# Casts and copies moved from GpSimd to VectorE and ScalarE, with a new order of all queues, in an attention and maxout kernel

## The chip, the cores and the metric

The kernel runs on one core of a Trainium2 chip. The metric is the time on the device in microseconds (us), the median of several runs; lower is better. The engines of the core are TensorE (PE in the profile; its weight loads have a row of their own, PEld), VectorE (DVE), ScalarE (ACT), GpSimd (POOL) and SyncE (SP), which only issues DMAs here. Each works through its own queue in order, and they wait for each other by semaphores.

## The reference, cut to what matters

```python
# attention, for 4 batches x 8 heads x 768 positions x 64
scores = (q @ k.T) / 8 + bias          # bias: -slope[head] * distance
keep   = (key < 8) | (0 <= query - key < 96)
a      = softmax(where(keep, scores, -1e9))
x      = (a @ v), heads side by side   # 3072 x 512
# maxout
h      = max(x @ w1, x @ w2, x @ w3)   # 3072 x 768
out    = h @ w_out                     # 3072 x 512, f32
```

A query sees the 8 first keys and the last 96 before it, so a tile of 128 queries needs the keys of its own tile, of the tile before it, and the 8 global ones. All inputs are f32 in HBM; the kernel computes in bf16 with f32 sums.

## The kernel before, in words

The 3072 positions are 24 tiles T of 128 (6 per batch); G is a pair of tiles. The tiles are put together to 7 chunks c of 4, 2, 2, 4, 4, 4 and 4 tiles (`SIZES`), and the maxout part runs over chunks. The whole program is one list, `SCHEDULE`, in which each word is a unit: a letter, its numbers, and after `@` the place in a ring of buffers (for units on PE the PSUM bank) that it takes. Line 571 goes through the list and emits each unit's instructions, so the order of the list is the order within each engine's queue; there is no other scheduling. A last number often names the engine: 0 ScalarE, 1 VectorE, 2 GpSimd (`copies`, line 190). The units are:

- `l` loads q, k or v of a pair of tiles (512 KB), with 12 as the pair's number for the first four tiles, in parts; `w` and `q` load weights; all on SP's queue
- `c` (L195 on VectorE and ScalarE, L201 in two halves on GpSimd) casts q or k to bf16; `v` (L254) casts one half of a tile's v; `W` and `Q` (L195, L201) cast weights
- `x` (L270, L276) transposes q or k by matmuls into PSUM, `y` (L283, L287) copies that out; `X` (L292) does both by a DMA
- `G` (L313, L315) and `V` (L321 to L325) put the 8 global keys and values into the rows of a tile that the next tile's queries no longer need; a `V` must come after the product `A` that reads the old rows. On GpSimd `V` copies 32-bit words, elsewhere bf16
- `S` (L349) scores, `e` (L356) exp from PSUM on ScalarE, `m` (L365, L367) product with a mask on VectorE. With `b` (L335) ahead of `S`, the bias is added by matmuls instead and there is no `m`; `B`, `K` and `R` make the bias and the masks at the start
- `A` (L391, L394) weights times v, with a column of ones that gives the sums; `n` (L402, L403) normalises on VectorE
- `t` (L418) and `u` (L421) transpose x by matmuls and copy it out; `Z` (L424) does it by a DMA
- `F` (L433) is one of 18 products per chunk (6 blocks f, 3 weights j), 4 matmuls each into one PSUM bank. `f` is its way out: j = 0 copies to bf16 (L447, ScalarE or VectorE), j = 1 and 2 take the maximum on VectorE (L449, L452)
- `O` (L457) is the last product of one tile, 6 matmuls of 512 columns; `o` (L471) copies it to SBUF, `s` (L477) stores it. `s` with a last number 2 stores in two halves
- `E` (L479 to L505) is the end of the last chunk in one unit: its four tiles with copies and stores, the last tile in parts of 256, 128 and 128 columns, the last of them stored from ScalarE's queue. Behind `E` the list has one more tile, `O5.0@2 o5.0.0@5 s5.0.2`
- `D` (L532) is matmuls on zeros whose result nobody reads: ten of 512 columns at the start, and three of 256 after the first transposes

`RINGS` says how many buffers each kind has; a unit that takes a place waits until the last readers of it are done.

Of the kernel before, what the change touches and what calls it, by code (L numbers as in the profile page):

```python
# [24 lines left out]
    l0.12.1@0 l1.12.1@1 D10.512@0 l1.12.3@2 l0.12.2@3 l0.12.3@4 R K7 K6 B1.1 K4 B2.1 K2 B3.0 K1 K5 B0.1 B6.1  # L25
    K0 c0.12.3.2@0 l1.12.2@5 c0.12.1.1 B4.1 B5.1 c1.12.1.1@1 K3 x12.0.1@0 y0.0.1.0@0 B7.1 l2.0.2@0 D3.256@1
    x12.1.1@1 b0.1@2 v1.0.2 l2.1.2@1 c1.12.3.1 v1.1.2 b1.0@4 y0.1.1.0 b1.1@6 S1.1.1 l0.2.2@6 c0.12.2.1
    y1.0.1.1@1 y1.1.1.0 x12.0.2@0 e1.1@0 c1.12.2.1 x12.0.3 y0.0.0.1 l1.2.2@0 y1.0.0.1 x12.1.3@1 x12.1.2
    y0.1.0.0 S0.1.1 e0.1@1 G0.1 b2.1@6 v2.0.2 v3.0.2 w1.0@0 S1.0.1 G1.0 e1.0@2 b2.0@2 w0.0@0 y1.1.0.1 S2.1.1
    w1.1@1 S0.0.0@0 e0.0@3 l2.2.2@2 S2.0.1 v0.0.1 e2.0@4 w0.1@1 v0.1.1 m0.0.1 e2.1@5 v2.1.2 b3.0@4 A1@0  # L30
    V1.1.1 V1.0.2 G2.1 v3.1.2 w0.2@2 A0@2 S3.0.1 e3.0@6 b3.1@6 n1@0 c0.2.2.2@2 S3.1.1 G3.0 A2@0 V2.0.2
    e3.1@7 V2.1.2 n0@1 t0@2 W0.0.2 c1.2.2.1 u0.0@0 x2.1.2@3 y2.1.2.0@2 w1.2@2 x2.0.2@2 A3@4 t1@6 u1.0 n2@2
    y2.0.2.1 t2@7 n3@3 l0.3.2@1 l1.3.2@2 S4.1.0@0 V3.1.2 e4.1@0 V3.0.2 S4.0.0@2 W1.1.2 u2.1 t3@6 G4.1 u3.0
    W2.0.1 S5.1.0@4 e5.1@2 S5.0.0@0 e5.0@1 m4.1.1 W1.0.1 e4.0@3 F0.5.0@7 F0.4.0@6 W2.1.0 F0.3.0@4 f0.3.0.0@0
    F0.2.0@5 f0.4.0.1@1 F0.1.0@6 v4.1.2 v4.0.2 l2.3.2@0 f0.1.0.0@2 q2@0 v5.1.0 F0.0.0@0 F0.5.1@1 F0.4.1@4
    F0.2.1@6 m4.0.1 f0.0.0.0@3 v5.0.0 f0.5.0.0@4 m5.1.1 A4@2 V4.1.0 F0.3.1@0 W0.1.2 f0.4.1.1 W0.2.0 m5.0.1
    f0.5.1.1 F0.0.1@1 F0.1.1@4 V4.0.1 W1.2.0 n4@1 t4@7 A5@2 W2.2.0 c1.3.2.2@0 f0.0.1.1 f0.1.1.1 F0.1.2@1
    n5@0 u4.1@1 f0.1.2.1@0 F0.0.2@4 q0@1 t5@7 u5.0 q1@2 f0.3.1.1 f0.0.2.1 F0.2.2@2 F0.3.2@3 f0.3.2.1
    c0.3.2.0 f0.2.0.0@2 f0.2.1.1 F1.2.0@4 F1.0.2@7 Q2.0 v7.1.2 F1.0.0@5 f1.0.0.1@3 v6.1.2 F1.0.1@3 f0.2.2.1
    f1.0.1.1 f1.2.0.1@0 Q0.2 f1.0.2.1@1 x3.1.2@6 y3.1.2.1@3 F0.4.2@5 f0.4.2.1 l1.4.2@3 v6.0.2 Q1.2 F1.1.0@0  # L40
    F1.2.2@1 l0.4.2@4 l1.6.2@5 F1.2.1@4 f1.2.1.1 F1.3.1@2 f1.2.2.1 F1.3.2@3 v7.0.2 F1.3.0@4 f1.3.0.0@2
    f1.3.1.1 f1.3.2.1 x3.0.2@1 F0.5.2@5 f0.5.2.1 F1.4.0@2 F1.1.1@3 f1.1.0.0@3 y3.0.2.0 S6.0.0@0 S6.1.0@4
    G6.2 c1.4.2.2@1 c0.4.2.2 l0.5.2@0 c0.5.2.2@2 f1.1.1.1 f1.4.0.0@1 e6.0@4 S7.0.0@6 S7.1.0@2 l1.5.2@6
    c1.5.2.2 e6.1@5 c1.6.2.2@0 e7.1@6 F1.4.1@0 e7.0@7 l2.4.2@1 O0.2@1 f1.4.1.1 m7.1.1 x4.1.2@0 F1.5.2@2
    F1.5.0@3 m7.0.1 v8.1.2 F1.5.1@4 A7@6 f1.5.0.1@0 m6.1.1 m6.0.1 o0.2.0@0 y4.1.2.0@0 f1.5.1.1 f1.5.2.1
    x4.0.2@3 y4.0.2.0 G7.0 l0.6.2@1 c0.6.2.2 F1.4.2@5 O0.1@4 f1.4.2.1 n7@2 o0.1.1@1 A6@0 l2.5.2@2 S8.1.0@2
    S8.0.0@6 n6@3 V7.1.1 G8.1 v8.0.2 F1.1.2@4 O0.3@5 t6@0 v11.0.2 v9.0.2 v9.1.2 f1.1.2.1 V7.0.0 t7@1 e8.1@0
    e8.0@3 S9.0.0@2 u6.0@2 S9.1.0@6 m8.1.1 u7.1 o0.3.0@2 O0.0@4 e9.1@1 m8.0.1 o0.0.0@3 e9.0@2 F2.4.0@5
    m9.1.1 f2.4.0.0@2 A8@0 V8.0.2 n8@1 F2.5.0@4 F2.2.1@6 f2.5.0.1@4 F2.1.0@7 f2.1.0.0@0 G9.0 F2.5.1@5 V8.1.2
# [15 lines left out]
    X16@1 o3.3.0@8 A15@0 n15@2 O3.0@7 S19.1.0@0 v17.1.1 m18.0.1 S16.1.0@2 m18.1.1 e19.1@1 S16.0.0@4 O3.2@6
    o3.0.1@9 e16.0@2 V15.1.2 A18@0 e16.1@6 n18@0 o3.2.1@10 m16.1.1 X17 O3.1@7 G16.0 Z14 o3.1.0@11 m16.0.1
    V15.0.1 S17.0.0@0 v16.0.0 Z12 S19.0.0@2 Z15 e19.0@7 S17.1.0@4 e17.1@0 m17.1.1 F4.4.0@6 e17.0@5 l0.11.2@1
    s1.0 l2.10.2@0 F4.2.0@7 l1.10.2@2 F4.1.0@2 F4.5.0@3 v16.1.0 F4.3.0@0 A16@4 f4.2.0.0@2 Z18@2 V16.1.2
    f4.3.0.0@0 v20.0.2 G18.0 F4.1.2@1 f4.1.0.1@3 c0.11.2.2@1 m17.0.1 v17.0.1 l2.11.2@2 n16@3 s3.1 f4.5.0.0@4
# [542 lines left out]
```

## Time and profile before

| what | value |
|---|---|
| median of 3 runs | 176.07 us (176.06 to 176.23) |
| span of the profiled execution | 174.8 us |
| PE busy | 165.9 us, 95% |
| VectorE busy | 131.9 us, 75% |
| ScalarE busy | 95.4 us, 55% |
| GpSimd busy | 54.7 us, 31% |
| HBM read and written | 25.17 MB and 6.29 MB |

The span runs from the first to the last instruction of one profiled execution; the time of a run has about 1.3 us more around it. A row of the groups reads: line, engine, operation, output<-input, shape, count | busy us, mean ns of one | idle time before them, with what ended it. Matmuls are pipelined, so their durations are longer than their spacing: PE's busy time tells where it has work, not how well it is used.

### The profile page before, as it was taken

What the parts mean: (1) busy time and instruction counts of PE and PEld (TensorE: products, weight loads), DVE (VectorE), ACT (ScalarE), POOL (GpSimd) and SP (SyncE); (2) the same over time, 40 slices, a digit from 0 to 9 for tenths busy, and PEclk for the clock granted to TensorE, in tenths of its full rate; (3) what the DMA queues carried; (4) which work ended last, traced back from release to release, by engine and by line L of the source; (5) the groups of instructions that cost most, each with busy time, mean ns of one, the idle gap of its engine ahead of it and who ended that gap; (6) DMA issues with size and microseconds to landing.
All of it is one profiled execution on the core that took longest, in us unless ns stands there. A gap on an engine that the chain in (4) does not pass through costs nothing.

```text
span 174.8 us, 3865 instructions
## 1 busy us (share of the span) xinstructions
PE 165.9 (95%) x1485; PEld 93.6 (54%) x1507; DVE 131.9 (75%) x268; ACT 95.4 (55%) x147; POOL 54.7 (31%) x99
## 2 busy tenths in 40 slices
PE   7997999999999999898999999999999999999991
PEld 2555745577676877544445545544445554444460
DVE  7889864988599897989898678899578993074910
ACT  5988897672868788440667688200345651402051
POOL 4049295057586717003730003240530000000000
PEclk9999999999999999999999999999999999999998
DMA  5999999999899899999996759998990046370035
GB/s 149 352 292 327 402 360 385 270 371 311 229 303 179 139 183 266 267 290 284 165 135 112 114 145 306 305 210 260 231 213 20 0 120 137 121 286 4 0 119 185
DMA packets 66403, 37.36 MB, mean 214 GB/s; under 512 B 24144, under 2 KB 61392, under 8 KB 66384
## 3 DMA queue, kind: packets, MB, share of 16 engines
q1 hardware_dynamic: 66240, 37.04, 83.3%
q8 instruction: 12, 0.20, 0.5%
q10 hardware_dynamic: 144, 0.07, 0.1%
q14 instruction: 7, 0.06, 0.1%
HBM read 25.17 MB, written 6.29 MB: 180 GB/s over the span
## 4 chain that ended last, share of the span: by engine, by line
PE 76%; DVE 10%; DMA 6%; ACT 3%; issue 2%; SPq 0%; DVEq 0%
PE psum L433 44%; PE psum L457 17%; PE psum L349 6%; DMA xT<-xb 3%; DMA rawqk<-in_k_dram 3%; DVE P L365 3%; PE psum L391 3%; PE psum L394 2%; PE psum L276 2%; DVE ht L452 1%; DVE xb L403 1%; ACT P L356 1%; PE psum L270 1%; DVE qb L195 1%; PE psum L335 1%
## 5 line engine op out<-in xcount | busy, mean ns | idle before, releaser
L433 PE MATMUL psum<-xT,w 128*128 128x512 bf16 (+1 forms) x491 | 97.5, 348 | 1.5 <-DMA xT<-xb 0.7
L433 PEld LDWEIGHTS <-w 128*128 128x128 bf16 x504 | 47.6, 98 | 42.9 <-DMA xT<-xb 0.9
L356 ACT ACTIVATE P<-psum 128x1024 bf16<-128x1024 f32 (+1 forms) x48 | 43.3, 954 | 10.4 <-PE psum L349 10.3
L449 DVE TENSOR_TENSOR h<-h,psum 128x512 bf16<-128x512 bf16 (+1 forms) x42 | 25.0, 605 | 15.9 <-PE psum L433 12.4
L457 PE MATMUL psum<-wo,ht 128*128 128x512 bf16 (+2 forms) x147 | 33.4, 362 | 0.5
L447 ACT CAST h<-psum 128x512 bf16<-128x512 f32 (+1 forms) x27 | 13.8, 523 | 33.1 <-PE psum L433 29.8
L452 DVE TENSOR_TENSOR ht<-h,psum 128x512 bf16<-128x512 bf16 (+1 forms) x42 | 26.2, 644 | 2.1 <-PE psum L433 0.9
L365 DVE TENSOR_TENSOR P<-P,wmask 128x1024 bf16<-128x1024 bf16 x34 | 25.2, 752 | 2.0 <-ACT P L356 1.7
L457 PEld LDWEIGHTS <-ht 128*128 128x128 bf16 x156 | 13.8, 98 | 13.5 <-DVE ht L452 0.2
L254 POOL CAST va<-rawv 64x512 bf16<-64x512 f32 x28 | 18.5, 668 | 4.8 <-DMA rawv<-in_v_dram 3.7
L323 POOL COPY va<-vaf 4x260 int32<-4x260 int32 x17 | 7.2, 424 | 34.9 <-PE psum L394 34.5
L403 DVE TENSOR_TENSOR xb<-psum,rz 128x512 bf16<-128x512 f32 x24 | 16.6, 692 | 0.8
L201 POOL CAST qb<-rawk 128x512 bf16<-128x512 f32 x12 | 7.5, 654 | 23.7 <-DMA rawk<-in_k_dram 23.7
L349 PE MATMUL psum<-qkT 64*128 64x128 bf16 x352 | 14.4, 217 | 0.5 <-DVE qkT L315 0.4
L391 PEld LDWEIGHTS <-P 128*128 128x128 bf16 x192 | 12.6, 97 | 3.2 <-ACT P L356 0.4
L349 PEld LDWEIGHTS <-qkT 64*128 64x128 bf16 x352 | 10.0, 94 | 7.9 <-issue 5.9
L391 PE MATMUL psum<-va,P 128*128 128x65 bf16 x160 | 12.7, 193 | 0.7 <-DVE ht L452 0.6
L447 DVE CAST h<-psum 128x512 bf16<-128x512 f32 (+1 forms) x15 | 9.1, 615 | 5.1 <-PE psum L433 5.1
L471 ACT COPY staging<-psum 128x512 f32<-128x512 f32 x14 | 8.2, 592 | 8.8 <-PE psum L457 8.8
L201 POOL CAST qb<-rawq 128x512 bf16<-128x512 f32 x14 | 8.9, 664 | 9.0 <-DMA rawq<-in_q_dram 5.0
L394 PEld LDWEIGHTS <-P 128*128 128x128 bf16 x160 | 10.5, 97 | 2.1 <-issue 0.7
L394 PE MATMUL psum<-va,P 128*128 128x65 bf16 x128 | 9.9, 193 | 0.0
(72 smaller groups left out, 120.6 us busy)
## 6 DMA issues: line engine op xcount, KB each, us to landing
rawv<-in_v_dram SPq DMA_DIRECT2D x12, 512.0 KB, 7.0
out_dram<-staging SPq DMA_DIRECT2D x21, 256.0 KB, 2.7
rawq<-in_q_dram SPq DMA_DIRECT2D x10, 512.0 KB, 7.1
rawk<-in_k_dram SPq DMA_DIRECT2D x10, 512.0 KB, 7.3
staging<-in_moe_w_dram SPq DMA_DIRECT2D x3, 1024.0 KB, 9.3
staging<-in_moe_w_dram SPq DMA_DIRECT2D x3, 512.0 KB, 8.8
staging<-in_moe_w_out_dram SPq DMA_DIRECT2D x3, 512.0 KB, 6.3
out_dram<-staging SPq DMA_DIRECT2D x5, 128.0 KB, 2.2
```

The costliest lines, as they stand in the source:

```text
L254: copies[how](heads(va(T))[64 * e:64 * e + 64, :, 0:D], src)
L349: nc.tensor.matmul(sp[:, hh, j2, ds], qT(T - ds, 1, hsl, jp), qT(T, 0, hsl, jp), start=not how, stop=True, skip_group_check=True)
L356: nc.scalar.activation(P[:, :, 0:n], sps[T, g].rearrange("p a b d n -> p (a b) d n")[:, :, 0:n], AF.Exp, bias=0.0, scale=scale)
L365: mul(P, P, wmask[:, g, :, 0:2])
L391: nc.tensor.matmul(o, P[:, i, 0], heads(va(T))[:, h], start=True, stop=(t == 0), skip_group_check=True)
L394: nc.tensor.matmul(o, P[:, i, 1], heads(va(T - 1))[:, h], start=False, stop=True, skip_group_check=True)
L403: nc.vector.tensor_tensor(out=x.rearrange("p (g h) d -> p g h d", g=2), in0=o4[:, :, :, 0:64], in1=rz[:, :, :, None].to_broadcast([128, 2, ...
L433: nc.tensor.matmul(ps, w123[f // 2][:, j, dm, (f % 2) * 128:(f % 2) * 128 + 128], xT[c][:, dm], start=(dm == 0), stop=(dm == 3))
L447: copies[how](h01, ps)
L449: nc.vector.tensor_max(h01s[c, f], h01s[c, f], ps)
L452: nc.vector.tensor_max(dst, h01s[c, f].rearrange("p (t e i) -> p t e i", e=2, i=64), ps.rearrange("p (t e i) -> p t e i", e=2, i=64))
L457: nc.tensor.matmul(po, ht[c][:, f, tt * 128:(tt + 1) * 128], wo[:, f, cols], start=(f == 0), stop=(f == NF - 1))
```

## The change

Every unit that named GpSimd now names VectorE or ScalarE, and the list is written anew from the first word to the last: loads, casts, transposes, products and stores come in another order and take other places. GpSimd keeps only what the setup does (iota and the identity). The count of units by letter is the same but for one more `b` (b0.0, so tile 0 loses an `m`), one `D` less, and the units of the end. By engine (ACT, DVE, POOL; before, then after):

| unit | before | after |
|---|---|---|
| `v` | 6, 10, 32 | 20, 28, 0 |
| `c`, whole (1024 columns) | 4, 3, 13 | 11, 9, 0 |
| `c`, of the first four tiles | 0, 5, 1 | 2, 4, 0 |
| `V` | 4, 11, 17 | 15, 17, 0 |
| `G` | 9, 8, 3 | 11, 9, 0 |
| `W` and `Q` | 5, 2, 5 | 7, 5, 0 |
| `u` | 6, 3, 0 | 3, 6, 0 |
| `f` with j = 0 | 27, 15, 0 | 29, 13, 0 |
| `o` (`E` apart) | 14, 6, 0 | 15, 11, 0 |

`E` is gone. `O` can now name a range of blocks f and of 64-column parts, `o` and `s` a range of parts, and the end is made of such units. The rings change as the diff shows. The diff, with the list cut to its first and last lines:

```diff
 SCHEDULE = """
-    l0.12.1@0 l1.12.1@1 D10.512@0 l1.12.3@2 l0.12.2@3 l0.12.3@4 R K7 K6 B1.1 K4 B2.1 K2 B3.0 K1 K5 B0.1 B6.1
-    K0 c0.12.3.2@0 l1.12.2@5 c0.12.1.1 B4.1 B5.1 c1.12.1.1@1 K3 x12.0.1@0 y0.0.1.0@0 B7.1 l2.0.2@0 D3.256@1
...
-    F6.5.0@1 f6.5.0.1@2 F6.5.2@5 f6.5.1.1 f6.5.2.1 E@7 O5.0@2 o5.0.0@5 s5.0.2
+    l0.12.1@0 l1.12.1@1 D10.512@0 l0.12.3@2 R B2.1 B5.1 B1.1 K6 K3 K0 K4 l1.12.2@3 K5 B3.0 B6.1 l1.12.3@4
+    c0.12.1.1@0 B4.1 x12.0.1@0 c1.12.1.1@1 B7.1 B0.1 K7 K2 c0.12.3.0 y0.0.1.0@0 K1 l0.12.2@5 l2.0.2@0 w0.0@0
...
+    o5.1.0@9 s5.1 o6.3.0.4.0@6 o5.2.1@10 s5.2 s6.3.0.4 O6.2@0 o6.2.0@5 s6.2 O5.0@1 o5.0.0@4 s5.0
 """
-RINGS = {'r': 7, 'rv': 3, 'qb': 3, 'qkT': 4, 'sp': 2, 'h': 8, 'P': 8, 'xb': 4, 'xT': 3, 'wst0': 3, 'wst1': 3, 'ht': 2, 'h01': 5, 'rz': 4, 'os': 12}
+RINGS = {'r': 7, 'rv': 3, 'qb': 2, 'qkT': 3, 'sp': 2, 'h': 8, 'P': 7, 'xb': 3, 'xT': 2, 'wst0': 3, 'wst1': 3, 'ht': 2, 'h01': 8, 'rz': 3, 'os': 12}
...
-    def u_O(slot, c, tt):
-        pos[c, tt] = ring("h", slot, [128, DM], FP32, "po")
-        f2_mm(pos[c, tt], c, tt, range(NF))
+    def u_O(slot, c, tt, f0=0, f1=NF, c0=0, c1=8):
+        if slot is not None:
+            pos[c, tt, c0] = ring("h", slot, [128, (c1 - c0) * 64], FP32, "po")
+        for f in range(f0, f1):
+            nc.tensor.matmul(pos[c, tt, c0], ht[c][:, f, tt * 128:(tt + 1) * 128], wo[:, f, c0 * 64:c1 * 64],
                              start=(f == 0), stop=(f == NF - 1))
+    def u_o(slot, c, tt, *rest):
+        c0, c1 = rest[:-1] or (0, 8)
+        osts[c, tt, c0] = ring("os", slot, [128, DM], FP32, "ost")[:, 0:(c1 - c0) * 64]
+        copies[rest[-1]](osts[c, tt, c0], pos[c, tt, c0])
+    def u_s(slot, c, tt, c0=0, c1=8, queue=0):
         T = chunks[c][tt]
+        (nc.sync, nc.scalar)[queue].dma_start(out=out[T * 128:(T + 1) * 128, c0 * 64:c1 * 64], in_=osts[c, tt, c0])
...
-    def u_E(slot):
...
```

The stretch of the new list up to its first products, of which the prediction speaks:

```
...
v3.1.0 S2.0.1 G2.0 b3.0@0 b3.1@4 S3.0.1 S3.1.1 e2.0@1 A2@6
V2.0.1 G3.1 V2.1.1 v3.0.0 e3.1@3 e3.0@0 x2.0.2@2 t0@3 y2.0.2.0@0 t1@4 u1.0@0 u0.0 c1.2.2.1 x2.1.2@5 n2@0
y2.1.2.1 A3@0 n3@1 S4.1.0@6 e4.1@0 S4.0.0@4 G4.1 t2@3 u2.1 e4.0@3 W2.0.0 t3@2 u3.1 S5.0.0@0 e5.0@1 S5.1.0@6
e5.1@2 F0.1.0@2 f0.1.0.0@0 v5.1.0 W1.0.1 F0.3.0@3 F0.0.0@4 f0.3.0.0@1 v4.1.1 v4.0.1 m4.0.1 V3.1.1 F0.5.0@5
...
```

More of the change, by code (lines that the diff above doesn't have):

```diff
@@ L30 @@
[L30 to L49, printed above, removed]
@@ L65 @@
[L65 to L69, printed above, removed]
@@ new lines @@
+    m19.0.1 A15@2 n15@0 Z15 V15.1.1 V15.0.0 O3.2@4 o3.2.1@0 v16.1.1 v17.0.0 S16.1.0@2 S16.0.0@0 O3.3@6 X21@0
+    o2.0.0@1 O3.0@7 e16.1@1 X20 l0.11.2@0 e16.0@2 G16.0 o3.0.0@2 S17.0.0@0 m16.1.1 v19.0.1 o3.3.1@3 l1.11.2@6
+    S19.1.0@2 e19.1@5 S17.1.0@4 e17.1@6 G18.0 G19.0 v18.0.1 m16.0.1 v18.1.1 s3.1 F4.5.0@6 F4.4.0@7 F4.2.0@2
+    f4.2.0.0@3 v16.0.1 A16@4 V16.1.0 e17.0@1 V16.0.0 m17.1.1 v19.1.1 m19.1.1 n16@0 s3.2 l2.11.2@0 F4.0.0@3
+    f4.4.0.1@0 f4.5.0.1@6 F4.1.0@2 A19@4 n19@1 Z19@1 f4.1.0.0@7 m18.1.1 F4.3.0@7 f4.3.0.0@1 F4.4.1@2 f4.4.1.1
@@ L133 @@
         chunks.append(list(range(first, first + n)))
-    last = len(chunks) - 1
     pools = {}
@@ L453, in u_f @@
                                  ps.rearrange("p (t e i) -> p t e i", e=2, i=64))
-    def f2_mm(po, c, tt, fs, cols=slice(0, DM)):
-        for f in fs:
-            nc.tensor.matmul(po, ht[c][:, f, tt * 128:(tt + 1) * 128], wo[:, f, cols],
-                             start=(f == 0), stop=(f == NF - 1))
-    def f2_out(po, ost, c, tt, copy, cols=slice(0, DM), dma=nc.sync):
-        T = chunks[c][tt]
-        copy(ost, po)
-        dma.dma_start(out=out[T * 128:(T + 1) * 128, cols], in_=ost)
```

118 lines of the change are left out of this document (50 added, 68 removed).

## The prediction

> **What bounds the kernel now.** I read the page first, then the sums by stretch, then TensorE's (PE's) own waits.
>
> ```profile
> span 174.8 us, 3865 instructions
> PE 165.9 (95%) x1485; PEld 93.6 (54%) x1507; DVE 131.9 (75%) x268; ACT 95.4 (55%) x147; POOL 54.7 (31%) x99
> ```
>
> ```profile
> core 0: us, PE busy (x) PEld busy (x) DVE busy (x) ACT busy (x) POOL busy (x), PEclk, DMA share, GB/s
> 0.00:22.00 22.00, 19.26 (x236) 11.35 (x238) 18.77 (x55) 18.38 (x31) 9.37 (x23) 1.00 1.01 305
> 22.00:62.00 40.00, 39.72 (x398) 26.44 (x403) 31.09 (x63) 28.78 (x44) 24.72 (x40) 1.00 1.05 280
> 62.00:125.00 63.00, 61.05 (x528) 33.02 (x536) 52.77 (x100) 31.88 (x49) 17.84 (x32) 1.00 1.00 219
> 125.00:165.00 40.00, 39.73 (x288) 19.54 (x292) 27.63 (x50) 13.53 (x20) 2.75 (x6) 1.00 0.39 108
> 165.00:175.00 10.00, 6.10 (x40) 3.23 (x39) 1.64 (x3) 2.88 (x6) 0.00 (x0) 0.92 0.37 133
> ```
>
> From 22 us to 165 us TensorE is busy for 140.5 of 143 us: it is the bound, and its matmuls are the same before and after the change. What can move is the time in which it has nothing to do. That is in three places: the first 22 us, where VectorE (DVE, 18.77) and ScalarE (ACT, 18.38) are both nearly full and the first product F waits for both; a few holes in the middle; and the tail after the last matmul. The two largest holes in the middle are these:
>
> ```profile
> PE psum L433 <- DMA xT<-xb: 0.7, 1, 0.7
> PE psum L391 <- DVE ht L452: 0.6, 1, 0.6
> ```
>
> The start ends here; the columns are start, length, instruction:
>
> ```profile
> 20.11 0.41 DVE L421 COPY xT<-psum 128x512 bf16<-128x512 bf16 x1
> 20.95 0.58 ACT L421 COPY xT<-psum 128x512 bf16<-128x512 bf16 x1
> 21.58 7.93 PE L433 MATMUL psum<-xT,w 128*128 128x512 bf16 x35
> ```
>
> The last transposed activations leave ScalarE at 21.53, and the first F starts 0.05 us later. So whatever is queued ahead of these copies on DVE and ACT sets the start of the long run of matmuls.
>
> **The change: what moves where.** GpSimd (POOL) loses all its work past the setup: 32 v casts, 13 c casts of q and k and one half, 5 weight casts, 17 V copies and 3 G copies. Durations:
>
> ```profile
> L254 DVE CAST va<-rawv 64x512 bf16<-64x512 f32 x8 | 3.4, 423 | 0.1
> L254 ACT CAST va<-rawv 64x512 bf16<-64x512 f32 x4 | 2.5, 618 | 0.0
> L195 DVE CAST w<-staging 128x1024 bf16<-128x1024 f32 x2 | 1.4, 686 | 0.0
> L195 ACT CAST w<-staging 128x1024 bf16<-128x1024 f32 x4 | 4.0, 1042 | 0.0
> L325 DVE COPY va<-vaf 4x520 bf16<-4x520 bf16 x11 | 4.2, 381 | 0.9 <-PE psum L394 0.8
> L325 ACT COPY va<-vaf 4x520 bf16<-4x520 bf16 x4 | 2.5, 621 | 7.9 <-PE psum L394 7.9
> L365 DVE TENSOR_TENSOR P<-P,wmask 128x1024 bf16<-128x1024 bf16 x34 | 25.2, 752 | 2.0 <-ACT P L356 1.7
> L421 DVE COPY xT<-psum 128x512 bf16<-128x512 bf16 x3 | 1.2, 412 | 0.0
> L421 ACT COPY xT<-psum 128x512 bf16<-128x512 bf16 x6 | 3.5, 585 | 3.0 <-PE psum L418 3.0
> L471 DVE COPY staging<-psum 128x512 f32<-128x512 f32 x6 | 4.1, 684 | 0.2 <-PE psum L457 0.2
> L471 ACT COPY staging<-psum 128x512 f32<-128x512 f32 x14 | 8.2, 592 | 8.8 <-PE psum L457 8.8
> L449 DVE TENSOR_TENSOR h<-h,psum 128x512 bf16<-128x512 bf16 (+1 forms) x42 | 25.0, 605 | 15.9 <-PE psum L433 12.4
> L356 ACT ACTIVATE P<-psum 128x1024 bf16<-128x1024 f32 (+1 forms) x48 | 43.3, 954 | 10.4 <-PE psum L349 10.3
> ```
>
> Counting letters in both queues, DVE gains 18 v (18 x 0.423 = 7.6), 6 c of a full 1024 columns less one half (3.7), 3 weight casts (2.1), 6 V (2.3), 3 whole o (2.1) and 3 u (1.2), and gives away 2 first maxout copies and 1 mask product (-1.7): +17.3 us. ACT gains 14 v (8.7), 7 full c (7.3) and two halves (1.2 by the 585 ns of a 512-wide copy), 11 V (6.8), 2 weight casts (2.1) and 2 maxout copies (1.0), and loses 3 o and 3 u (-3.6): +23.5 us.
>
> **What DVE gets back.** While POOL reads SBUF, the mask product can be held up:
>
> ```profile
> 107.98 0.61 POOL L254 CAST va<-rawv 64x512 bf16<-64x512 f32 x1 [0.18 <-DMA rawv<-in_v_dram]
> 108.54 1.16 POOL L201 CAST qb<-rawq 128x512 bf16<-128x512 f32 x2
> ```
>
> ```profile
> 108.19 2.86 DVE L365 TENSOR_TENSOR P<-P,wmask 128x1024 bf16<-128x1024 bf16 x2
> ```
>
> Two products take 2.86 us there, just as long as POOL is at work, and
>
> ```profile
> L365 DVE TENSOR_TENSOR P<-P,wmask x34: 672/685/2058, 21.1 to 141.5; 128x1024 bf16<-128x1024 bf16 x34
> ```
>
> says that the median is 685 and the longest 2058. Mean less median gives 34 x 0.067 = 2.3 us; I take 4 us for all kinds together, between 2.3 and the 5 us that it would be if V copies and early casts lose as much again. So DVE goes from 131.9 to about 145 us, ACT from 95.4 to about 119. [...]
>
> **The first stretch (0 to 22 us).** Up to its last copy of x transposed, DVE's queue now holds one c cast of k or q more (0.69) and one quad half less (-0.42), 3 v (1.27), 3 V (1.14, or 0.86 without POOL beside them), W0.0 (0.69), one u (0.41), one y (0.69) and one G (0.2) more, and one mask product less (-0.4): +4 us on a queue that ended at 20.52. DVE was idle for 22 - 18.77 = 3.2 us of the stretch, into which some of this can fit, at most about 2.3 (the rest lies before its first instruction); of the 4 us of locks, POOL's share of busy time here (9.37 of 54.68) gives 0.7. Bounds: 20.5 + 4 - 2.3 - 0.7 = 21.5, and 20.5 + 4 - 0.7 = 23.8. On ACT, two quad halves (1.2) and 3 v (1.9) are new, an exp (-0.95), a u (-0.6) and a y (-0.6) are gone: +0.9 on a copy that ended at 21.53, which gives 22.4 where it finds no idle time. I take 22.3, just under ACT's 22.4 and near the middle of DVE's bounds: first F **+0.7 us** (-0.1 to +2.2).
>
> ```profile
> 16.54 0.73 DVE L195 CAST qb<-rawk 128x1024 bf16<-128x1024 f32 x1
> ```
>
> On the DMA queue w0.0 (512 KB) now stands ahead of the last q, k and v of this stretch: at 305 GB/s they land 1.7 us later. Behind the cast c1.2.2 on DVE stand n2, n3, u2 and u3, so F would wait; that cast ran at 16.54 without a wait, its data can be there by 18.2, and DVE reaches it at about 19 (22.3 less these four). Hidden, by 0.8 us. The extra bias unit b0.0 is two short matmuls (+0.2 with what it delays); three fill-in matmuls go, which nothing waits for.
>
> **The second stretch (first F to 62 us).** PE's units here come to the same work, some 38 us. DVE holds 9 v (3.8), 4 c (2.7), 4 weight casts (2.7), 6 V (2.3), 2 mask products (1.5) more and about 3 maxout steps less (-1.9): +11 on 31.09 busy us, less 1 to 2 of locks: **40 to 41 us of work in 40 us**. ACT goes to 28.8 + 4 = 33. Back to back, instructions overlap a little, and eight PSUM banks let PE run some F ahead, so a full DVE is no stall by itself; but the 9 us in which it could wait for exp results or matmuls are gone, and each wait is handed on to PE. Bounds: nothing, if the order never leaves DVE waiting, and 4 us, if it waits half as long as it did. I take **+1.2 us**, nearer to nothing because the banks stand between.
>
> **The third stretch (62 to 125 us).** DVE +9 - 2 = 59.5 of 63 us; ACT gains 9 V (5.6), 7 v (4.3), 4 c (4.2), 5 exps that the new order puts here (4.8): 52 of 63. PE lost 1.95 us here, 1.25 in the two named holes, both behind a DVE queue that locks had lengthened. I take **-0.7 us**: the holes go in part, the load is higher (-1.4 to +1.5). New waits: V must wait for the products A that read the old rows.
>
> ```profile
> POOL va L323 <- PE psum L394: 34.5, 7, 10.4
> ACT va L325 <- PE psum L394: 7.9, 2, 6.7
> ```
>
> On POOL these 34.5 us had only other casts behind them; on ACT and DVE the exps, first copies h and maxout steps stand behind a V, and PE waits for them. I cost this at nothing beyond the terms above, since in the queue each V stands behind its A. The rings of xb, xT, qb and qkT lose a place each: n15 must wait until the transposing DMA of tile 14 has read its buffer, with m and f steps behind it on DVE.
>
> ```profile
> xT<-xb SPq DMA_TRANSPOSE x15, 3.4
> ```
>
> Ahead of n15 stand about six DVE units, some 4 us, which cover 3.4; without that cover it is 1 us or so.
>
> **The tail.** The change speaks of a 128-column part last, but both queues end with O5.0, its ScalarE copy and its store; the 128-column part of tile 23 now comes some 12 units before the end. Only the halving of the last store goes:
>
> ```profile
> 171.80 0.81 SPq L477 DMA_DIRECT2D out_dram<-staging x2
> ```
>
> ```profile
> out_dram<-staging SPq DMA_DIRECT2D x21, 256.0 KB, 2.7
> ...
> out_dram<-staging SPq DMA_DIRECT2D x5, 128.0 KB, 2.2
> ```
>
> Before: 171.80 + 0.41 + 2.2 = 174.4; one store of 256 KB: 171.80 + 2.7 = 174.5. **Nothing** (-0.1 to +0.5).
>
> **The sum.** +0.7 + 0.2 + 1.2 - 0.7 + 0 = +1.4 on the profiled span of 174.8, so 176.2; 176.07 - 174.8 = 1.3 us lie around the span in the median of the runs shown, so **177.5 us**. Lowest ends: -0.1 + 0 + 0 - 1.4 - 0.1 = -1.6, 174.5; highest: 2.2 + 0.2 + 1.8 (all ends do not come together: of the 4 + 1.5 of the later stretches I take a third) = +4.2, 180.3.
>
> **Rivals.** *A, VectorE stays the bound into the third stretch* (0.17): the stretch at 40 to 41 of 40 us starts late, its backlog isn't worked off at 94% load, and V waits at the head of ACT's queue hold up exps: 0.7 + 0.2 + 2.0 in the second and 0.8 in the third stretch = +3.7, 179.8. For it speaks the load; against it that the banks have hidden most of DVE's waits so far (PE 39.72 of 40). *B, faster, by the end of the locks* (0.26): place: the start, 66 to 83 and 107 to 111 us; price: the 4 us of locks, of which the 1.25 us of holes have reached PE, and little at the start: 176.07 - 1.2 = 174.9. It decides once the first F starts no later than 21.6 and DVE's work in the second stretch comes in order without waits. Against it: 17 us of new work for 4 us of locks. *C, no difference* (0.08): late start and filled holes cancel: 176.1. *D, the clock* (0.03):
>
> ```profile
> 5.47 0.94 PE L270 MATMUL psum<-identb,qbq 128*128 128x128 bf16 x8
> 6.25 0.49 PE L532 MATMUL psum<-zeros 128*128 128x256 bf16 x3
> 6.99 0.62 PE L270 MATMUL psum<-identb,qbq 128*128 128x128 bf16 x8 [0.25 <-DVE qbq L195]
> ```
>
> Eight transposes take 0.94 us, later ones 0.62, and the three matmuls on zeros between them are removed. If PE fell back to the slow rate in that hole, each early group of transposes would cost 0.32 more; with two such groups ahead of F that is +0.6 beyond the forecast, 178.1. [...] The forecast has the rest, 0.46.
>
> **Range and chances.** 174.5 to 180.3 takes in B and A; outside it lie the worst of A and a B that also shortens the start. A measurement of this kernel tells about 0.2%, 0.35 us, from no change. Faster is B, 0.26; same is C, 0.08; slower is the forecast, A and D, 0.66.
>
> **What would show it.** No POOL instruction beyond the setup; mask products all near 0.69; DVE about 145 and ACT about 119 busy us; first F at 22.0 to 23.0; in 22 to 62 us DVE over 37 us busy and PE with holes that wait for DVE or ACT; the tail 3.6 us after the last matmul as now. I am wrong if the first F starts before 21.6, or if PE's holes between 22 and 125 us stay under 2 us although DVE is full.

## The result and the profile after

The kernel after takes **181.27 us** (median of 4 runs, 180.79 to 183.29) against 176.15 before: 1.0327 times as long, 95% interval 1.0267 to 1.0386. The forecast of 177.5 had the sign, but the time lies 1 us above the top of its range. Runs far above the fastest of the same kernel are left out of all ratios here, so a median can stand higher than its ratio says.

The profiled execution of after took 180.79 us. From its page: the span, the busy time by engine, the shares of the chain that ended last, and the mask products.

```profile
span 179.0 us, 3802 instructions
...
PE 166.4 (93%) x1484; PEld 93.3 (52%) x1506; DVE 141.8 (79%) x305; ACT 118.0 (66%) x180; POOL 1.8 (1%) x9
...
PE 68%; DVE 12%; DMA 11%; issue 3%; SPq 3%; ACT 0%; DVEq 0%
...
L358 DVE TENSOR_TENSOR P<-P,wmask 128x1024 bf16<-128x1024 bf16 x34 | 22.5, 684 | 2.7 <-ACT P L349 2.5
```

The change did what it says. GpSimd has only its setup left, VectorE has 10 us more work and ScalarE 22.6, and the mask products went from a mean of 752 to 684 ns, the longest from 2058 to 694: the delays beside GpSimd's work, which the prediction calls locks, are gone. TensorE has the same work, in a span 4.2 us longer. Its busy time by stage (stretch, length, PE, PEld, DVE, ACT, POOL, clock, DMA) stands beside the table that the prediction shows of before:

```profile
0.00:22.00 22.00, 17.28 (x210) 9.99 (x210) 18.57 (x57) 18.48 (x33) 1.76 (x9) 1.00 1.00 290
22.00:62.00 40.00, 39.63 (x393) 25.14 (x395) 37.33 (x84) 34.26 (x46) 0.00 (x0) 1.00 1.01 287
62.00:125.00 63.00, 59.41 (x571) 33.66 (x579) 54.09 (x110) 50.07 (x79) 0.00 (x0) 1.00 0.99 205
125.00:165.00 40.00, 39.74 (x262) 19.33 (x266) 27.74 (x50) 12.55 (x20) 0.00 (x0) 1.00 0.34 106
```

PE is 2.0 us less busy in the first stretch (17.28 against 19.26, of which 0.5 are the matmuls on zeros that the change takes out), level in the second although VectorE is full there, and 1.6 us less busy in the third. Busy time is no measure of progress, so the same can be counted in columns of matmuls done, from the traces: at 0.216 us for 512 columns, after lies some 1.6 us behind before from 22 to 70 us (1.3 to 2.0), 3.0 at 82 us, 3.9 at 110 us, and no further from there on. So the loss has two places, the start and the stretch from 78 to 110 us. The first F starts here:

```profile
23.40 1.47 PE L426 MATMUL psum<-xT,w 128*128 128x512 bf16 x5
```

That is 1.8 us later than before (21.58). In the third stretch PE's waits have two new heads, at 82 and at 106 us:

```profile
PE psum L384 <- DVE h L442: 1.7, 1, 1.7
...
PE psum L426 <- DVE P L358: 1.1, 1, 1.1
```

The first of them can be followed back by hand. First PE, then VectorE's queue in front of it:

```profile
77.78 2.75 PE L426 MATMUL psum<-xT,w 128*128 128x512 bf16 x12
82.25 0.20 PE L384 MATMUL psum<-va,P 128*128 128x65 bf16 x1 [1.72 <-DVE h L442]
```

```profile
74.86 0.42 DVE L442 TENSOR_TENSOR h<-h,psum 128x256 bf16<-128x256 bf16 x1
78.61 0.42 DVE L247 CAST vaf<-rawv 64x512 bf16<-64x512 f32 x1 [3.33 <-DMA rawv<-in_v_dram]
79.05 0.43 DVE L360 TENSOR_TENSOR P<-P,wmask 128x512 bf16<-128x512 bf16 x1
79.39 1.29 DVE L358 TENSOR_TENSOR P<-P,wmask 128x1024 bf16<-128x1024 bf16 x2
...
81.17 0.43 DVE L360 TENSOR_TENSOR P<-P,wmask 128x512 bf16<-128x512 bf16 x1
81.51 0.68 DVE L442 TENSOR_TENSOR h<-h,psum 128x512 bf16<-128x512 bf16 x1
```

The cast v12.1 stands at the head of VectorE's queue and waits 3.33 us for its load. Four mask products and a maximum that PE needs stand behind it. Before, that cast was on GpSimd. How GpSimd's queue waited for loads in the kernel before:

```profile
POOL qb L201 <- DMA rawk<-in_k_dram: 23.7, 5, 10.1
POOL qbq L201 <- DMA rawqq<-in_q_dram: 5.9, 1, 5.9
POOL qb L201 <- DMA rawq<-in_q_dram: 5.0, 4, 2.1
...
POOL va L254 <- DMA rawv<-in_v_dram: 3.7, 5, 1.9
```

With its other waits that is 85 us, and nothing but casts and copies stood behind them. These rows suggested the theory that most runs below try: **what costs is less the work than the waits that came with it** (W). Its rival is the work itself (L).

### The profile page after: what moved, and what is told of

It is laid out like the page before. It is cut to its first block, busy times and chain, and to the rows that moved or that the text cites. A ratio compares the mean times of both kernels' runs of the same rounds, so it can differ in the third digit from the quotient of the medians.

```text
span 179.0 us, 3802 instructions
## 1 busy us (share of the span) xinstructions
PE 166.4 (93%) x1484; PEld 93.3 (52%) x1506; DVE 141.8 (79%) x305; ACT 118.0 (66%) x180; POOL 1.8 (1%) x9
## 4 chain that ended last, share of the span: by engine, by line
PE 68%; DVE 12%; DMA 11%; issue 3%; SPq 3%; ACT 0%; DVEq 0%
PE psum L426 44%; PE psum L453 13%; DMA rawv<-in_v_dram 11%; PE psum L342 4%; PE psum L384 3%; PE psum L387 2%; DVE ht L445 2%; SPq L222 2%; DVE h L442 2%; DVE va L247 2%; DVE P L358 1%; PE psum L269 1%; DVE qb L188 1%; DVE xb L396 1%; DVE vaf L247 1%
## 5 line engine op out<-in xcount | busy, mean ns | idle before, releaser
L426 PE MATMUL psum<-xT,w 128*128 128x512 bf16 (+1 forms) x489 | 99.0, 348 | 1.9 <-DVE P L358 1.1
L453 PE MATMUL psum<-wo,ht 128*128 128x512 bf16 (+2 forms) x149 | 32.7, 362 | 0.5 <-issue 0.2
L459 ACT COPY staging<-psum 128x512 f32<-128x512 f32 (+1 forms) x15 | 8.4, 573 | 27.4 <-PE psum L453 23.7
L358 DVE TENSOR_TENSOR P<-P,wmask 128x1024 bf16<-128x1024 bf16 x34 | 22.5, 684 | 2.7 <-ACT P L349 2.5
L440 ACT CAST h<-psum 128x512 bf16<-128x512 f32 (+1 forms) x29 | 14.6, 523 | 8.3 <-PE psum L426 4.5
L318 ACT COPY va<-vaf 4x520 bf16<-4x520 bf16 x15 | 9.3, 621 | 5.4 <-PE psum L387 5.2
L440 DVE CAST h<-psum 128x512 bf16<-128x512 f32 (+1 forms) x13 | 7.9, 622 | 5.6 <-PE psum L426 5.6
L247 ACT CAST va<-rawv 64x512 bf16<-64x512 f32 x18 | 11.1, 619 | 0.3
L459 DVE COPY staging<-psum 128x512 f32<-128x512 f32 (+1 forms) x11 | 6.5, 613 | 4.6 <-PE psum L453 2.2
L247 DVE CAST va<-rawv 64x512 bf16<-64x512 f32 x22 | 9.3, 423 | 0.5 <-DMA rawv<-in_v_dram 0.2
```

The source lines that it names most:

```text
L247: copies[how](heads(va(T))[64 * e:64 * e + 64, :, 0:D], src)
L358: mul(P, P, wmask[:, g, :, 0:2])
L426: nc.tensor.matmul(ps, w123[f // 2][:, j, dm, (f % 2) * 128:(f % 2) * 128 + 128], xT[c][:, dm], start=(dm == 0), stop=(dm == 3))
L440: copies[how](h01, ps)
L453: nc.tensor.matmul(pos[c, tt, c0], ht[c][:, f, tt * 128:(tt + 1) * 128], wo[:, f, c0 * 64:c1 * 64], start=(f == 0), stop=(f == NF - 1))
```

## The experiments

Each ratio is to the kernel before on the same chip. The first four expectations were written before W and L had their names and explain their own theories.

| run | median us | ratio (95%) | span, profiled |
|---|---|---|---|
| e1 engines alone | 196.52 | 1.116 (1.111 to 1.121) | 194.7 |
| e2 order alone | 185.19 | 1.052 (1.045 to 1.059) | 182.0 |
| e5 the 44 that never waited | 188.59 | 1.072 (1.066 to 1.078) | 185.7 |
| e6 the 27 that waited | 189.55 | 1.078 (1.074 to 1.082) | 187.9 |
| e4 one load early | 182.35 | 1.026 (1.021 to 1.031) | 178.7 |
| e7 two loads early | 180.93 | 1.026 (1.019 to 1.032) | 181.6 |
| e8 three casts on GpSimd | 182.56 | 1.034 (1.027 to 1.042) | 178.7 |
| e10 third stretch | 181.61 | 1.027 (1.019 to 1.036) | 177.6 |
| e13 third stretch, n15 | 180.14 | 1.020 (1.013 to 1.027) | 178.6 |
| e3 start on GpSimd | 182.45 | 1.037 (1.033 to 1.040) | 181.2 |
| e12 first weight later | 185.15 | 1.053 (1.046 to 1.061) | 182.8 |
| e14 e12 and e13 together | 184.68 | 1.048 (1.041 to 1.055) | 182.6 |
| e15 both at the start | 184.01 | 1.046 (1.042 to 1.050) | 182.1 |
| e17 all | 182.85 | 1.036 (1.028 to 1.044) | 179.2 |
| e18 all, q2 with its own buffer | 179.91 | 1.022 (1.018 to 1.025) | 177.7 |
| e16 before, three casts moved | 176.30 | 1.002 (1.000 to 1.004) | 174.2 |

### The two halves of the change (e1, e2)

e1 is the kernel before with 71 units on the engines that after gives them; e2 is after with the same 71 back on GpSimd.

```diff
-v1.0.2 V1.0.2 c1.3.2.2@0
+v1.0.1 V1.0.1 c1.3.2.0@0
```

> The kernel before, with its own order, rings and end, but each of the 71 units that named GpSimd on the engine that the changed kernel gives it (VectorE or ScalarE). Theory Q (casts and copies do harm at the head of queues that TensorE needs, where they wait for loads and for products): 181 to 186 us, with idle VectorE or ScalarE in front of v, c and V, as the order was not made for it. Rival O (the new order is what costs, the engines are nearly free because the locks go): 175.5 to 177.5 us.

> The changed kernel with its new order, rings and end, but the 71 units that were GpSimd's in the kernel before are GpSimd's again. Theory Q: the holes of TensorE near 80 and 105 us shrink or go and the first product starts near 22.0: 176 to 178.5 us. Rival O (the order costs): 180 to 181.5 us, the holes stay where they are.

Both theories missed both runs. The engines alone cost 20.5 us, more than any estimate, and the order alone 9.2; together they cost 5.1. So the new order belongs to the new engines: it gives back some 15 of the 20.5 us, and it is bad for the old ones. At the start of e1 the granted clock is lower too: 1.00 from 10 to 20 us in before, where PE is busy for 8.98 of the 10 us, and 0.66 in e1:

```profile
10.00:20.00 10.00, 6.80 (x69) 4.04 (x69) 6.09 (x14) 5.85 (x11) 0.00 (x0) 0.66 1.14 335
```

### Waits or work (e5, e6)

The 71 units of e1, split by whether GpSimd waited at that unit in the profile of before.

> The kernel before, in its old order. Of its 71 casts and copies on GpSimd, only the 44 that began there without a wait (29 us of work: 27 v, 10 V, 3 c and 4 others) go to the engines that the kernel after gives them; the 27 that waited there stay. All 71 moved cost 20.5 us. Theory W (what costs is that a cast that waits for its load, or a V that waits for PE, now stands at the head of the queue of VectorE or ScalarE; on GpSimd it held up nobody): 176 to 179.5. Theory L (what costs is the work itself on VectorE and ScalarE): the share of 29 in 52 us of work, about 11 us, so 184 to 190.

> The counterpart: the kernel before, in its old order, with only the 27 casts and copies moved that waited on GpSimd (85 us of waits in the profile of before; some 22 us of work: 11 c, 7 V, 5 v and 4 others). Theory W: nearly all of the 20.5 us, so 189 or more. Theory L: the share of 22 in 52 us of work, about 9 us, so 182 to 187.

e5 costs 12.6 us, e6 13.6. By the times alone, e5 speaks for L and e6 for W. But the units were sorted by their waits in the old queue, and a unit that didn't wait there can wait in a new one. The v of tile 1 comes in one load and is cast in two halves. In before the first half waited for that load on GpSimd, and the second, right behind it, had nothing left to wait for. e5 moves the second alone, to VectorE. First GpSimd in before, then VectorE and PE in e5:

```profile
11.18 1.37 POOL L254 CAST va<-rawv 64x512 bf16<-64x512 f32 x2 [1.91 <-DMA rawv<-in_v_dram]
```

```profile
11.07 0.43 DVE L248 CAST va<-rawv 64x512 bf16<-64x512 f32 x1 [3.55 <-DMA rawv<-in_v_dram]
...
12.90 1.78 PE L264 MATMUL psum<-identb,qbq 128*128 128x128 bf16 x16 [3.89 <-DVE qkT L277]
```

Now the cast waits 3.55 us at the head of VectorE's queue, PE waits 3.89 us for a copy behind it, and PE's granted clock is 0.92 in the first 22 us and 0.96 from 22 to 62 us (before: 1.00 in both). At its first F, PE in e5 is already 8.5 us later than in before, of 10.9 at the end of the two profiles. So most of e5's loss starts with a wait for a load, and **e5 doesn't tell W from L**. What the work alone costs, no run here shows. (12.6 and 13.6 are more than 20.5, so the two don't add.)

### The hole at 82 us (e4, e7, e8)

Three ways of ending the wait of v12.1, the first two with the load, the last with the engine:

```diff
 # e4, e7: the load ahead of two transposing DMAs
+l2.6.2@0 Z8@1
-... Z9 l2.7.2@1 l2.6.2@0
 # e7 also: k of tiles 16 and 17 right behind the cast that frees its buffer
+c1.9.2.0@0 l1.8.2@4
 # e8 instead
-v12.1.1 c0.9.2.0 c1.8.2.0
+v12.1.2 c0.9.2.2 c1.8.2.2
```

> The changed kernel with one word of the list moved: the load of v for tiles 12 and 13 stands 11 units earlier, ahead of the transposing DMA Z8, on SP's queue. Theory Q: VectorE's wait of 3.3 us for that load at 75 to 78.6 us goes, and with it TensorE's hole of 1.7 us at 80 to 82: 1.3 to 2.0 us less, about 179.5. Rival B (VectorE is overfull anyway, so the hole only moves): within 0.5 us of the changed kernel.

> The kernel after, with two loads earlier in the list: v of tiles 12 and 13 ahead of Z8, and k of tiles 16 and 17 right behind the cast that frees its buffer. In the profile of after VectorE waits 3.33 us and ScalarE 3.42 us for these two. Theory W: both waits and the two PE holes behind them, at 80 and at 105 us (1.9 and 1.3 us), go: 2 to 3 us less than after, 178 to 179. Theory L: as with the first load alone other holes open in their place: 180.2 or more.

> The kernel after, with its loads where they are and three of its casts back on GpSimd: the three that wait 3.3, 3.4 and 0.8 us for their loads (v of tile 12, second half; k of tiles 16 and 17; q of tiles 18 and 19). Only 2.5 us of work leave VectorE and ScalarE. Theory W: as with the early loads, 178 to 179.2, since GpSimd can wait without holding up a step that PE needs. Theory L: 2.5 us of 260 us of work are nothing, 180.3 to 181.3.

In all three the wait and the hole at 82 us are gone: set against after, PE gains 1.9 to 2.2 us between 79 and 84 us in the same list. So the cause of this hole is **shown**, from both sides. GpSimd again waits at no cost; the first row of its queue in e8:

```profile
79.28 0.78 POOL L245 CAST vaf<-rawv 64x512 bf16<-64x512 f32 x1 [76.65 <-DMA rawv<-in_v_dram]
```

But only 0.3 us is left at the end of e4 and e8 (spans of 178.7 and 179.0), and the medians of the three (182.35, 180.93, 182.56) reach what W expected in none of them. PE's next two waits in e4 are

```profile
75.27 1.02 PE L424 MATMUL psum<-xT,w 128*128 128x512 bf16 x4 [0.88 <-DVE h L440]
...
106.09 2.10 PE L424 MATMUL psum<-xT,w 128*128 128x512 bf16 x9 [1.43 <-DVE P L356]
```

The first is made by the edit. The transposing DMA Z9 now stands behind the moved load: it lands at 75.18 us (73.19 in after), and F starts 0.09 us later. (F starts as soon behind Z9 in e7 and e10, which move the same load, so the engine that the row names isn't what it waited for.) e8 moves no load and has no such wait. The second is a limit that PE's gain doesn't move: the last transposing DMA ahead of chunk 4, Z15, lands at 106.00 us in e4, 106.03 in e8 and 106.38 in after, and F starts 0.09 us behind it each time. To that extent the rival was right: this limit stood there already.

e7's profile (183.36 us, the longest of its four runs) shows one more thing. The columns of the windows are as above; the eighth number is the clock.

```profile
104.00:106.00 2.00, 1.30 (x27) 0.70 (x25) 0.00 (x0) 1.54 (x3) 0.00 (x0) 1.00 1.41 81
106.00:108.00 2.00, 0.86 (x3) 0.39 (x4) 1.91 (x4) 1.38 (x4) 0.00 (x0) 0.87 1.18 223
108.00:110.00 2.00, 2.00 (x6) 0.73 (x5) 1.94 (x5) 0.00 (x0) 0.00 (x0) 0.50 0.78 108
110.00:112.00 2.00, 2.00 (x21) 1.07 (x21) 0.76 (x2) 0.39 (x1) 0.00 (x0) 0.78 1.06 311
```

```profile
107.14 4.44 PE L424 MATMUL psum<-xT,w 128*128 128x512 bf16 x12 [1.83 <-DVE staging L457]
```

The same twelve matmuls in e8, behind as long a hole:

```profile
106.12 2.75 PE L424 MATMUL psum<-xT,w 128*128 128x512 bf16 x12 [1.84 <-DVE staging L457]
```

In e7 they take 4.44 us, in e8 2.75: **behind this hole e7 lost nearly as much again**, 1.69 us, with a granted clock of 0.50 from 108 to 110 us. The two holes are equally long (1.83 and 1.84 us), but e8's clock is 1.00 from 62 to 125 us and e7's 0.97. Why it fell in the one and not in the other, no run here shows. The order of after scatters in its clock too: its four runs have spans of 179.0 to 181.5 at clocks of 1.00 to 0.98.

### The hole at 105 us (e10, e13)

F of chunk 4 waits for the last two transposing DMAs, Z13 and Z15. They are issued at 100.2 to 102.9 us in after, behind a v load and behind n15; Z15 lands at 106.38, and F starts at 106.47. PE's row above names VectorE, the row of the weight loads names the DMA:

```profile
PEld L426 <- DMA xT<-xb: 1.3, 1, 1.3
```

e10 moves six words; e13 also changes one digit.

```diff
 # e10, with the loads of e7
-Z12@0 ... m15.0.1 Z13 ... G15.1 c0.10.2.1 ... m19.0.1 A15@2 n15@0 Z15
+l2.9.2@1 Z12@0 Z13 ... m15.0.1 ... G15.1 ... A15@2 n15@0 Z15 c0.10.2.1 m19.0.1
 # e13
-n15@0
+n15@1
```

> The kernel after, with seven words moved and no work changed: the v loads of tiles 12 and 18 and the k load of tiles 16 earlier, Z13 right behind Z12, and c0.10.2.1 and m19.0.1 behind n15 and Z15, so that the last two transposing DMAs that F of chunk 4 needs start earlier. Theory W: the holes at 80 and 105 us both go (1.9 and 1.3 us), and the wait at 75 to 79 with them: 177 to 178.5. Theory L: other holes of the same size open, 180 or more.

> The run with the third stretch mended, with one more digit changed: n15 takes place 1 of the ring of xb instead of place 0. There n15 on VectorE waited 1.57 us for the transposing DMA that still read its buffer (a ring of 3 places, 4 before), and PE 1.34 us behind it. Theory W: wait and hole go, 1 to 1.4 us less in the profiled span (177.6 to about 176.4), and with fewer holes fewer executions with a halved clock: median 178 to 180. Theory L: span 177.3 or more, median over 180.5.

e10's profile gains 1.4 us (177.6), its median nothing. Behind the mended hole stood the ring of xb, first on VectorE, then on PE:

```profile
99.79 0.69 DVE L394 TENSOR_TENSOR xb<-psum,rz 128x512 bf16<-128x512 f32 x1 [1.57 <-DMA xT<-xb]
```

```profile
100.54 0.62 PE L340 MATMUL psum<-qkT 64*128 64x128 bf16 x16 [1.34 <-DVE xb L394]
```

In e13 both are gone, and the scores wait for X instead:

```profile
PE psum L340 <- DMA qkT<-qb: 1.4, 2, 1.0
```

e13's span (178.6) is what L expected of it, and its median (180.14) lies between the two theories. Each repair ends its own wait, and the next limit stands close behind it.

### The start (e3, e9, e12, e15)

> The changed kernel, but the 12 casts and copies ahead of the first product F that GpSimd did in the kernel before are GpSimd's again (10 off VectorE's or ScalarE's queue at the start; one half c, two weight and k or q casts, five v, three V). If VectorE's added work is why the first F starts at 23.40 and not 21.58: first F at 22.0 to 22.5 and 1 us less, about 180.2. If the later landing of the loads sets it: first F stays at 23.0 to 23.5 and the time within 0.4 us.

> The kernel after, with the load w0.0 behind the k load of tiles 2 and 3, and its cast W0.0 behind that k's cast on VectorE. In the profiles of after's order that k load lands at 18.0 to 18.4 us, in some executions at 19.5, against 16.44 before; in the latter VectorE waits 1.23 us for it and PE's clock halves for some us behind the hole. Theory W (a cast stands at the head of its queue, waiting for its load): first F 1 to 1.5 us earlier, and the slow executions go: median 179.0 to 180.0. Theory L (VectorE's work ahead of F is too much): the same work stands ahead of F, so the first F is no earlier, and the time is 180.4 to 181.5 as after.

> The kernel after, with the load w0.0 behind the k load of tiles 2 and 3, the cast W0.0 behind that k's cast on VectorE, and the load q2, which takes W0.0's buffer, behind the cast. (The run before it with this edit left q2 in place: the cast then read what q2 loaded, so its weights were others, and it waited for that load; its 202.7 us answer nothing.) Theory W (load order: a cast at the head of VectorE's queue waits for its load): first F 1 to 1.5 us earlier, 179 to 180. Theory L (VectorE's work ahead of F): the same work stands there, first F as in after, 180.4 to 181.6.

> The kernel after with the first stretch relieved in both ways at once: the twelve units ahead of the first F that were on GpSimd before are there again, and the load w0.0 stands behind the k load of tiles 2 and 3 (W0.0 last on GpSimd, q2 behind it, Q2 on ScalarE some steps later). With the twelve on GpSimd alone that k landed at 18.1 us and its cast had to wait for it; with the load order alone the k landed at 16.66 and the cast waited for VectorE's queue until 17.92. Theory LW (both limits stand at 18 us, and either alone hides the other): the cast at 16.7 to 17.2 us, first F 1 to 1.4 us earlier than in those two, at 21.6 to 22.2. Theory R (the new order of PE's queue is what makes F late): first F at 22.5 or later.

```diff
 # e3: twelve units ahead of F
-v1.1.1 v1.0.1 ... W0.0.1 ... V1.0.1 ... v2.1.1 v2.0.1 ...
+v1.1.2 v1.0.2 ... W0.0.2 ... V1.0.2 ... v2.1.2 v2.0.2 ...
 # e12 (e9 without the move of q2, so with other weights in place of W0.0)
-l2.0.2@0 w0.0@0 l2.1.2@1 ... l1.2.2@4 ... W0.0.1 ... q2@0 ... c1.2.2.1
+l2.0.2@0 l2.1.2@1 ... l1.2.2@4 w0.0@0 ... c1.2.2.1 W0.0.1 q2@0
 # e15: e3 and e12 together, Q2 on ScalarE
```

What counts is the cast of k of tiles 2 and 3, the head of the chain to F (from the traces, us):

| run | k landed | cast started | first F |
|---|---|---|---|
| before | 16.44 | 16.54 | 21.58 |
| after | 18.38 | 18.86 | 23.40 |
| e4 (same start as after) | 18.03 | 18.26 | 22.79 |
| e8 (same start as after) | 19.49 | 19.51 | 24.04 |
| e3, twelve on GpSimd | 18.11 | 18.13 | 22.96 |
| e12, load earlier | 16.66 | 17.92 | 23.85 |
| e15, both | 16.56 | 16.59 | 22.05 |

In e3 the cast waits for the load. Its first F is near where the later landing would have it, but its time of 182.45 is 1.2 us over after's and outside both theories: PE falls back 0.9 us near 46 us, the hole at 82 is 2.16 us long, and the granted clock is 0.97 from 62 to 125 us (1.00 in after). In e12 it waits for VectorE's own queue, which is at work without a break until 17.92. **Two limits stand at 18 us, and each hides the other**; only e15 lifts both and brings F to 22.05, as its theory LW said. (e9 took 202.74 us and answers nothing: with q2 left in place, W0.0 waited for it and read its values. So did e11, e9 with the words of e10, which took 201.47.) e12 and e15 are slower overall for a reason of the edit: W0.0 and q2 now wait in turn at the heads of other queues, 1.89 us for q2 in e12:

```profile
19.56 0.69 DVE L186 CAST w<-staging 128x1024 bf16<-128x1024 f32 x1 [0.95 <-DMA staging<-in_moe_w_dram]
...
43.05 0.69 DVE L186 CAST wo<-staging 128x1024 bf16<-128x1024 f32 x1 [1.89 <-DMA staging<-in_moe_w_out_dram]
```

The table shows two more things. 0.5 us of after's late first F belongs to its one profiled execution, whose first load landed at 5.24 us; in the other profiles of after's order it landed between 4.58 and 4.91, but for 5.17 in e18. And the k load lands a further 1.4 us later in some executions of the same list (e8), which VectorE then waits for.

### All of it, and the kernel before (e14, e17, e18, e16)

> Both edits together, start and third stretch. Theory W: they add, 176.5 to 178.5, near the kernel before, with a granted clock of 0.995 or more in all runs, since no hole of over 1 us is left. Theory L: 179.5 or more.

> The kernel after with the start of the run e15 and the third stretch of the run e13. If the order of loads, rings and the twelve units at the start explain the whole loss: 176 to 178 and a granted clock of 0.995 or more. If VectorE's and ScalarE's work in the third stretch is itself a limit: 178.5 or more.

> The run with everything mended, with the fault of that edit taken away: q2 is loaded at its old place in the list into a fourth buffer of its ring, so that it need not wait for W0.0, and Q2 is where the kernel after has it. In the two runs before, PE had a hole of 2.1 to 2.4 us at 43 us from that. If order, rings and twelve start units explain the loss: profiled span 176.5 to 177.5, median 177.5 to 179.5, that is 2 to 4 us less than after. If other holes open in its place, as VectorE's and ScalarE's load would have it: span 178.5 or more, median 180 or more.

```diff
 # e17: e15 and e13 together. e18, against e17:
-W0.0.2 q2@0 ... y3.0.2.0 Q2.0
+q2@3 ... W0.0.2 ... Q2.1 ... y3.0.2.0
-'wst0': 3
+'wst0': 4
```

e14 and e17 carry the wait for q2, in e17 a hole of 2.1 us at 43 us, and so neither theory is tried by their times. e18 takes it away: 1.022 (1.018 to 1.025) lies below after's interval, so a third of the loss goes with all these edits together. e13, without those at the start, has as little (1.020, 1.013 to 1.027). e18's profile came in at 177.7, just above W's interval, its median in between the two theories. Where the gain at the start went:

```profile
24.00 0.86 DVE L245 CAST va<-rawv 64x512 bf16<-64x512 f32 x2 [1.06 <-DMA rawv<-in_v_dram]
24.78 0.68 DVE L356 TENSOR_TENSOR P<-P,wmask 128x1024 bf16<-128x1024 bf16 x1
25.49 0.60 DVE L316 COPY va<-vaf 4x520 bf16<-4x520 bf16 x2
26.02 1.88 DVE L356 TENSOR_TENSOR P<-P,wmask 128x1024 bf16<-128x1024 bf16 x3
```

F starts 1 us earlier, but the v of tiles 4 and 5 lands at 24 us as in after, VectorE waits 1.06 us for it and is then full, and at 30 us PE stands where it stood in after, within 0.1 us. So the earlier first F gives nothing here: VectorE's work and that load hold PE behind it. The stretch from 22 to 30 us, before and then after:

```profile
22.00:30.00 8.00, 7.99 (x51) 3.91 (x51) 4.11 (x7) 6.54 (x10) 6.71 (x10) 1.00 1.09 373
```

```profile
22.00:30.00 8.00, 7.95 (x73) 4.19 (x69) 7.66 (x18) 7.90 (x10) 0.00 (x0) 1.00 1.07 368
```

VectorE goes from 4.11 to 7.66 of 8 us: nothing is left there to take up a late load.

> The kernel before, with three GpSimd casts on ScalarE: the two of v of tile 12, moved to a stretch in which ScalarE waits for PE, and k of tiles 14 and 15 in its place. They ran beside VectorE's mask products at 66 to 70 us and beside its cast of 1.13 us (others 0.69) at 80 us, ahead of PE's holes at 72 and 82 us. If those locks made the holes: 0.5 to 1.2 us less, 175.0 to 175.7. If not, or if ScalarE's own queue then holds up a step: 176 to 177.

```diff
-v12.1.2 v12.0.2 ... c0.9.2.0@2 ... c1.7.2.2
+... c0.9.2.0@2 v12.1.0 v12.0.0 ... c1.7.2.0
```

e16 tries less than it set out to. The mask products at 66 to 70 us took 0.68 to 0.70 us in before too, so no lock stood there; the hole at 72 us ended with the landing of a transposing DMA (72.77, F at 72.81), which lands at 71.56 in e16. Only the cast at 80 us took longer, beside GpSimd's casts of k from 79.94 to 81.57 us: 1.13 us, 0.69 in e16. Both holes are gone (PE's longest wait past the start is now 0.3 us), the profiled span is 0.6 us shorter than that of before, and the time is no less: 1.002, 1.000 to 1.004. The holes may belong to the profiled execution of before, which by its span was one of the longer ones (174.8; the seven runs of before beside e1 to e4 have 173.6 to 174.8). No version beats the kernel before.

## Why the prediction was wrong

The forecast of 177.5 is 3.8 us too low: 2.8 in the profiled span (179.0 for 176.2), 0.5 in what lies around the span, and 0.5 because the median run of after is longer than the profiled one (181.27 and 180.79). Within the span the third stretch is off by 2.3 us and the first F with b0.0 by 0.9, the second stretch by 1.2 the other way; that these cancel in part is luck. The other 0.8 stands in none of these terms.

- **Third stretch, -0.7 us: the step that failed.** It measured +1.6 us of PE's busy time, just outside its bounds (-1.4 to +1.5). It counted two holes of before as the work of locks and so as a gain. The one at 72 us was the landing of a DMA, only the one at 82 us stood behind a locked cast, and e16, in which both are gone, is no faster. Of new waits it weighed that of a V for PE, "at nothing", from the row of 34.5 us, and n15's for its ring. The rows of 43 us in which GpSimd waited for loads stood in the same view, and were not used: for every cast that moves, the question was whether its load is there when its new queue reaches it. Where it wasn't, PE lost 1.7 us (e4, e7 and e8 end it), and 1.1 us more where Z15 came late. The price set for n15 was near (1 us without its cover, 1.57 measured in e10), but in after the cover held.
- **First F, +0.7 us.** +1.8 in the profile, of which 0.5 is that execution's first load; +1.1 to +1.4 in e4, e10 and e13, which have the same start: within its bounds, but half too small. In e8 and e7, where the k load landed at 19.5 us, it is +2.5 and +3.5, outside them. VectorE reached the cast of k about where it was expected (at 18.86 in after, for "about 19"). "Hidden, by 0.8 us", of the load order, was thin: 0.48 us in after (18.38, 18.86), nothing in e8.
- **Second stretch, +1.2 us.** PE's busy time is the same within 0.1 us (39.63 and 39.72), with VectorE at 37.33 of 40. That the banks hid it, as the argument beside the term said, fits, but no run tries it.
- **Locks, 4 us.** Too small, and of no use. The mask products gave back 2.7 (25.2 to 22.5), near the 2.3 read for them. But V copies went from a mean of 381 to 282 ns and casts of k from 932 to 685, and over all kinds the means differ by some 5.6 us, more than the 5 set as the most. That is part of why VectorE's 141.8 lies under the forecast's 145. What delays VectorE beside GpSimd, no run shows; they show that the same operations took less time without GpSimd's work.
- **Tail and b0.0.** As forecast: 4.0 us from the start of the last matmul to the end in both profiles.
- **1.3 us around the span.** Mis-sized: it is 1.79 in after's profiled run, and 1.7 to 1.9 in runs of before with known spans (176.04 with 174.3, 176.6 with 174.7). By these figures the profiled execution of before (174.8) took about 176.6, half a microsecond over the median run; taking its span with the median's time lost that.
- **Rivals.** A was nearest (179.8) with a wrong mechanism: PE left the second stretch no further behind than it entered it. B falls with after itself: the locks went, and the time rose. D's place was wrong: the second eight transposes took 0.62 us in before (at 6.99 us) and in after (at 7.50), so the added 0.32 is not there. A lower clock shows in other runs (e7: 0.50 from 108 to 110 us, behind a hole of 1.83 us), and what brings it about is not shown.

**What stays open.** e18 still loses 2.2% to before. By columns of matmuls done, 1.9 us of that is lost in the first 30 us and about 1 us more in the third stretch. How much of it another order could give back, and how much is VectorE's and ScalarE's load, no run here separates; e5, which was to do so, doesn't. The v load of tiles 4 and 5 ahead of w1.0 wasn't tried.

## What to carry to other kernels

Before work is moved from an idle engine, read what that engine's queue *waits* for. Here 85 us of waits on GpSimd had nothing but casts and copies behind them, while one wait of 3.33 us at the head of VectorE's queue left PE waiting for 1.72 us. Ask it of each unit in its new place: one that never waited in the old queue may have stood behind one that did (v of tile 1, 3.55 us in e5). When a repaired hole gives back less than its length, look for the limit that stands at the same time, and lift both in one run. GpSimd's 53 us of work were worth keeping here: with them elsewhere the time was 3% longer in after and 12% in e1.

## What the runs showed of the hardware

Behind a hole of 1.83 us, TensorE's granted clock in e7 was 0.87, 0.50 and 0.78 in the three stretches of 2 us from 106 us on, and twelve matmuls of F took 4.44 us. Behind one of 1.84 us in e8 the clock was 1.00 (62 to 125 us) and the same twelve took 2.75 us. With GpSimd's work gone, mask products took 684 ns on average for 752, V copies on VectorE 282 for 381. The load of k landed at 18.38 us in after and 18.03 in e4, and at 19.49 in e8, with the same list ahead of it.
